# Operand sums of seven half-size products moved from GpSimd to VectorE and made earlier; weight splits moved ahead of conversions

## The chip, the cores and the metric

The kernel runs on one core of a Trainium2 chip. The metric is device time in microseconds (us) for one execution. PE is TensorE's matmul side, PEld its weight loads, DVE is VectorE, ACT is ScalarE, POOL is GpSimd, SP is the engine whose queue issues the transfers.

## The reference

Four sequences of 448 rows pass through an attention of 12 heads with two mixing matrices over the heads, and its result x (4 x 448 x 768) through a mixer:

```python
xt = x.transpose(0, 2, 1)
h = np.maximum(xt @ w_tok1, 0.0) @ w_tok2          # mixes the 448 rows
u = x + h.transpose(0, 2, 1)
h2 = np.maximum(u @ w_ch1, 0.0) @ w_ch2            # 768 -> 1536 -> 768
return (u + h2)
```

The four weights come as 64-bit floats. Only the last two products, with `w_ch1` and `w_ch2`, are touched here. Over the 4 x 448 = 1792 rows they are done in two ways: the first 768 rows directly, the last 1024 by seven half-size products in place of eight (a scheme of the Strassen and Winograd kind).

## The kernel before, in words

**Exactness.** TensorE multiplies rounded operands. Every operand is therefore kept as a pair: a rounded high part, made by a copy on ACT, and a low part, source minus high part, made by a subtraction on DVE or POOL. One product is three matmuls (`mm3`, L653 to L655): high x high, weights' high x data's low, weights' low x data's high. In the rows `wh`, `wl` are the two parts of weights and `uh`, `ul`, `rh`, `rl` those of data.

**Conversion of weights.** The 64-bit weights are turned into 32-bit ones by `cv_tick`, one unit of 128x384 at a time: absolute value on ACT (L432), clamp on POOL (L438), three bit operations on DVE (L456, L460, L466). `split` (L404) then makes the pair of 128x768 weights; if the units that it needs aren't converted yet, it runs their ticks first.

**The direct passes (L889 to L921).** Outer loop g: pass 0 has 512 rows, pass 1 has 256. Inner loop c over 12 slices of the hidden size 1536: `ch1(g, c)` is six `mm3` into `pc`, followed by relu and split of the result on ACT (`rh`, L649) and DVE (`rl`, L650); `ch2(g, c - 1)` is six more `mm3`, into six accumulators `po`. Number n = 2c is the weight pair of `ch1`, n = 2c + 1 that of `ch2`; a pair has the slot n mod 6, and its split waits until the product six numbers earlier has been done. In pass 0 the odd-numbered splits are on POOL. Conversions run only in pass 0.

**The seven products (L922 to L933).** The 1024 rows are cut into two halves, the weights into quadrants A, the data into quadrants B. There are 28 stages of 27 matmuls each (nine `mm3` of 512 columns): stages 0 to 13 are the first layer (twice the seven products in the order 1, 5, 6, 3, 7, 2, 4), stages 14 to 27 the second (each product in two parts). Products 5, 6, 3, 7 need a sum or difference of two weight quadrants (128x1152), products 5, 6, 7, 4 one of two data quadrants (128x1536). Most are made in place, in `wt`, `us` or `rr`. `prep_s(n)` issues for stage n the sums (POOL, L809), the two roundings (ACT, L835) and the two low parts (DVE, L836). High and low parts lie in one of three slots, n mod 3. The loop issues `prep_s(n + 2)`, then the matmuls of stage n, then its eviction: ACT copies, or three DVE adds (L886, L877), the former followed by relus on ACT (L864) at the head of the next turn. `prep_s(0)` and `prep_s(1)` are issued near the end of pass 1.

**Order of the work.** Every engine takes its instructions in the order in which the code issues them, and an instruction that waits holds all that are behind it on its engine. There is no scheduler.

Of the kernel before, what the change touches and what calls it, by code (L numbers as in the profile page):

```python
# [14 lines left out]
ALU = mybir.AluOpType  # L15
# [16 lines left out]
NC = DC // 128  # L32
# [7 lines left out]
def attn_mixer_kernel(  # L40
# [12 lines left out]
    nc = tc.nc  # L53
# [17 lines left out]
    def close(*names):  # L71
        for n in names:
            opens.pop(n).release()
# [23 lines left out]
    for b in range(B):  # L97
        for t in range(4):
            n = IT[t][1]
# [39 lines left out]
    def pair(tag, name):  # L139
        return (ps if tag == "pre" else ps_w).tile([128, 2, 512], F32, tag=tag, bufs=2, name=name)  # L140
# [144 lines left out]
    p = pair("w", "pw")  # L285
# [4 lines left out]
    for x in range(2):  # L290
        ps_ = slice(64 * x, 64 * x + 64)
        nc.vector.tensor_tensor(
            out=kpre[ps_, :60].rearrange("p (i g) -> p i g", i=5),
            in0=kcat[0][ps_, :12].unsqueeze(1).to_broadcast([64, 5, H]),
            in1=mask[0][ps_, 5 * x:5 * x + 5].unsqueeze(2).to_broadcast([64, 5, H]), op=ALU.mult,
# [3 lines left out]
    for s in range(2):  # L299
        ps_ = slice(64 * s, 64 * s + 64)  # L300
        for hf in range(2):
            nc.gpsimd.tensor_tensor(
                out=kpost[ps_, 32 * hf:32 * hf + 30].rearrange("p (g i) -> p g i", g=6),
                in0=kcat[1][ps_, 12 + 6 * hf:18 + 6 * hf].unsqueeze(2).to_broadcast([64, 6, 5]),
                in1=mask[1][ps_, 5 * s:5 * s + 5].unsqueeze(1).to_broadcast([64, 6, 5]), op=ALU.mult,
# [96 lines left out]
    SP, split_at = {}, [0]  # L402

    def split(eng):  # L404
        n = split_at[0]
        split_at[0] += 1
        c, w = divmod(n % (2 * NC), 2)
        while cv_pos[0] <= min(4 * c + 2 * w + 5, len(units) - 1):
            cv_tick(1)
        src = WT[w, c // 3][:, c % 3, :]  # L410
        hi, lo = [y[:, :768] for y in wslot(n % 6)]
        nc.scalar.copy(out=hi, in_=src)
        eng.tensor_tensor(out=lo, in0=src, in1=f32(hi), op=ALU.subtract)  # L413
        SP[n] = (hi, lo)

    def wslot(i):
        p = prep["wr"] if i < 3 else prep["wx"]
        return [p.tile([128, 1152 if i < 3 else 768], F32R, tag=f"w{y}{i}", name=f"w{y}") for y in "hl"]

    def xslot(i):  # L420
        return [prep["ub"].tile([128, 1536], F32R, tag=f"u{y}{i}", name=f"u{y}") for y in "hl"]

    def cv_load(i):
        src, P, n, _ = units[i]
        r = prep["cv"].tile([128, n, 2], I32, tag="cv_r", bufs=5, name="cv_r")
        nc.sync.dma_start(out=r[:P], in_=src.rearrange("p (n two) -> p n two", two=2))
        raws[i] = r

    def cv_abs(i):
        _, P, n, _ = units[i]  # L430
        g = prep["cv"].tile([128, n], F32, tag="cv_g", bufs=3, name="cv_g")
        nc.scalar.activation(out=g[:P], in_=f32(raws[i])[:P, :, 1], func=ACTF.Abs)  # L432
        mags[i] = g

    def cv_clamp(i):
        P = units[i][1]
        g = mags[i]
        nc.gpsimd.tensor_scalar(  # L438
            out=g[:P], in0=g[:P], scalar1=MAG_MIN, scalar2=MAG_MAX, op0=ALU.max, op1=ALU.min,
        )  # L440
# [30 lines left out]
    def cv_tick(k, eng=nc.gpsimd):  # L471
        for _ in range(k):
            i = cv_pos[0]
            if i >= cv_lim[0]:
                return
            if i + 5 < len(units):
                cv_load(i + 5)
            cv_step(i, eng)
            if 0 <= i + 2 < len(units):
                cv_clamp(i + 2)  # L480
            if 0 <= i + 3 < len(units):
                cv_abs(i + 3)
            cv_pos[0] += 1
# [9 lines left out]
    for T in range(NT - 1):  # L493
        J = (sl[T] + 1) // 2
        n = sf[T + 2] // 2 - J
        if sf[T + 2] % 2 and sf[T + 2] // 2 > (sf[NT - 1] - 8) // 2:
            n += 1
        n = min(3, n)
# [4 lines left out]
    for T in range(2, NT):  # L503
        hi = (sf[T] - 8) // 2
        lo = max((sl[T - 2] - 8) // 2 + 1 + (T == 4), hi - 2)
# [146 lines left out]
    def mm3(p, a, x, first, last, on=False):  # L652
        nc.tensor.matmul(out=p, lhsT=a[0], rhs=x[0], start=first, stop=False, skip_group_check=on)  # L653
        nc.tensor.matmul(out=p, lhsT=a[0], rhs=x[1], start=False, stop=False, skip_group_check=on)  # L654
        nc.tensor.matmul(out=p, lhsT=a[1], rhs=x[0], start=False, stop=last, skip_group_check=on)  # L655
# [125 lines left out]
    def ch2(g, c, ds=range(KD)):  # L781
        i0, n = CB[g]
        ws = SP[2 * NC * g + 2 * c + 1]
        for d in ds:
            if c == 0:
                OP[g, d] = psb.tile([128, 512], F32, tag=f"o{d}", name=f"po{d}")
            mm3(OP[g, d][:, :n], [w[:, 128 * d:128 * d + 128] for w in ws], RL[g, c], c == 0, c == NC - 1)
            if c == NC - 1:
                o = UR[g][:, d, :n]
                nc.vector.tensor_tensor(out=o, in0=OP.pop((g, d))[:, :n], in1=o, op=ALU.add)  # L790
                o_row[0] = d
                store_out(i0, o)


    HN = (B * S - SB0) // 2
    ORDER = [1, 5, 6, 3, 7, 2, 4]
    stages = [(0, g, p, 0) for g in range(2) for p in ORDER] + [(1, 0, p, h) for p in ORDER for h in range(2)]
    SX, SW = {}, {}
# [6 lines left out]
        t, d = (us, 3 * j) if L == 0 else (rr, 6 * j + 3 * s)  # L805
        return t[:, d:d + 3, HN * k:HN * k + HN]

    def sum_(out, in0, in1, op=ALU.subtract):
        nc.gpsimd.tensor_tensor(out=out, in0=in0, in1=in1, op=op)  # L809

    def prep_s(n):
        L, g, p, h = stages[n]
        whi, wlo = [y.rearrange("p (a n) -> p a n", a=3) for y in wslot(n % 3)]
        xhi, xlo = [y[:, :3 * HN].rearrange("p (a n) -> p a n", a=3) for y in xslot(n % 3)]
        s = g if L == 0 else h
        A = {(i, j): a_q(L, i, j, s) for i in range(2) for j in range(2)}
        Bq = {(j, k): b_q(L, j, k, h) for j in range(2) for k in range(2)}
        tmp = rr[:, 6 + 3 * g:9 + 3 * g, :HN] if L == 0 and p in (7, 4) else None
        w, x = {1: (A[0, 0], Bq[0, 0]), 2: (A[0, 1], Bq[1, 0]), 3: (A[0, 0], Bq[1, 1]), 4: (A[1, 1], tmp or Bq[1, 0]),
                5: (A[1, 0], Bq[0, 1]), 6: (A[1, 0], Bq[0, 1]), 7: (A[1, 0], tmp or Bq[0, 0])}[p]  # L820
        if p == 5:
            sum_(w, A[1, 0], A[1, 1], ALU.add)
            sum_(x, *((Bq[0, 1], Bq[0, 0]) if L or g == 0 else (Bq[1, 1], Bq[0, 1])))
        elif p == 6:
            sum_(w, A[1, 0], A[0, 0])
            sum_(x, Bq[1, 1], Bq[0, 1])
        elif p == 3:
            sum_(w, A[0, 1], A[1, 0])
        elif p == 7:
            sum_(w, A[1, 1], A[1, 0])  # L830
            sum_(x, Bq[0, 1], Bq[0, 0])
        elif p == 4:
            sum_(x, Bq[1, 0], Bq[0, 1])
        for hi, lo, src in ((whi, wlo, w), (xhi, xlo, x)):
            nc.scalar.copy(out=hi, in_=src)  # L835
            nc.vector.tensor_tensor(out=lo, in0=src, in1=f32(hi), op=ALU.subtract)  # L836
        SW[n], SX[n] = (whi, wlo), (xhi, xlo)

    PB = {}

# [25 lines left out]
    def evict(n):  # L866
# [5 lines left out]
        for m in range(3):  # L872
# [12 lines left out]
            else:  # L885
                nc.vector.tensor_tensor(out=o, in0=ps_, in1=o, op=ALU.add)  # L886
                RELU.append(o)

    for g in range(2):  # L889
        for c in range(NC):  # L890
            ch1(g, c)
            cv_tick(3)
            if g == 0 and c == NC - 3:
                cv_tick(1000)
                close("cv", "a1")
                usp = en("us", bufs=1, side="right")
                urp = en("urp", bufs=1)
                us = usp.tile([128, KD, 2 * HN], F32, name="us")
                load_u(0)
                load_u(1)  # L900
                nc.sync.dma_start(out=us, in_=u_dr[:, :, SB0:])
            if c and (g == 0 or c < NC - 1):
                ch2(g, c - 1)
            while split_at[0] < min(2 * (NC * g + c) + 6, 4 * NC):
                split(nc.gpsimd if g == 0 and split_at[0] % 2 else nc.vector)
            if g and c == NC - 2:
                prep_s(0)
        if g == 0:
            n = CB[1][1]
            U[1] = [y[:, :KD * n] for y in xslot(2)]  # L910
            hi, lo = [y.rearrange("p (d n) -> p d n", d=KD) for y in U[1]]
            nc.scalar.copy(out=hi, in_=UR[1])
            nc.vector.tensor_tensor(out=lo, in0=UR[1], in1=f32(hi), op=ALU.subtract)
            ch2(g, NC - 1)
        else:
            prep_s(1)
            ch2(g, NC - 2, (0, 1))
            for d in range(KD):
                ch2(g, NC - 1, (d,))
                if d + 2 < KD:  # L920
                    ch2(g, NC - 2, (d + 2,))  # L921
    close("psb", "urp", "ob", "wx")  # L922
    rp = en("rr", bufs=1)
    rr = rp.tile([128, NC, 2 * HN], F32, name="rr")
    pss = en("pss", bufs=1, space=PSUM)
    for n in range(len(stages)):
        relus()
        if n + 2 < len(stages):
            prep_s(n + 2)
        mm_s(n)  # L930
        evict(n)
        if n == 13:
            nc.sync.dma_start(out=us[:, :3, HN:], in_=u_dr[:, :3, SB0 + HN:])  # L933
# [39 lines left out]
```

## Time and profile before

| | us |
|---|---|
| median of 3 runs | 743.91 (742.12 to 745.80) |
| the profiled execution: device time | 742.89 |
| its span, first to last instruction | 741.1 |
| PE busy in the span | 709.5 (96%) |
| DVE busy | 596.1 (80%) |
| POOL busy | 446.4 (60%) |
| ACT busy | 392.9 (53%) |

The stretches that matter here, counted from the start of the span: pass 0 from 386 to 488, pass 1 from 488 to 540, the seven products from 540 to the end. A matmul's end is modelled in the trace and overlaps the next one, so on PE the distance from start to start tells more than the busy time.

### The profile page before, as it was taken

The numbers are of one execution on the slowest core, as the hardware profiler recorded it, in microseconds if no ns is written. First come the engines' busy times: TensorE is split into PE (matmuls) and PEld (weight loads), VectorE is DVE, ScalarE is ACT, GpSimd is POOL, SyncE is SP. The second block draws the span as 40 slices with busy tenths as digits, with TensorE's granted clock in tenths as the row PEclk, the third lists the DMA queues.
The fourth block names the chain that finished last, engine by engine and source line by source line (L and its number), as shares of the span: only waits on it lengthen the run. The fifth ranks groups of instructions, "written<-read, shape, count | busy, mean of one in ns | idle before, by whom it ended". The sixth has DMA issues, their size and how long they took to land.

```text
span 741.1 us, 19026 instructions
## 1 busy us (share of the span) xinstructions
PE 709.5 (96%) x7688; PEld 491.0 (66%) x7688; DVE 596.1 (80%) x832; ACT 392.9 (53%) x751; POOL 446.4 (60%) x291
## 2 busy tenths in 40 slices
PE   8999999999999999999999999999999979897997
PEld 4244454445445344699997888899987757685786
DVE  4777777787767879797888999865789789899992
ACT  3676666666676575464424444444554554634240
POOL 3555656665656678665657999611297297299330
PEclk9999999999999999999999999999999999999999
DMA  6788688577757644746764556750010001000022
GB/s 181 244 233 222 216 223 228 178 225 225 217 187 237 204 145 156 268 147 205 253 201 140 149 149 171 239 188 2 1 42 1 1 0 43 0 1 0 11 75 86
DMA packets 72023, 105.47 MB, mean 142 GB/s; under 512 B 23123, under 2 KB 59520, under 8 KB 71936
## 3 DMA queue, kind: packets, MB, share of 16 engines
q1 hardware_dynamic: 71360, 103.35, 45.0%
q8 instruction: 61, 1.00, 0.5%
q10 hardware_dynamic: 480, 0.87, 0.5%
q14 instruction: 26, 0.21, 0.1%
q0 software_dynamic: 96, 0.03, 0.0%
HBM read 49.18 MB, written 16.52 MB: 89 GB/s over the span
## 4 chain that ended last, share of the span: by engine, by line
PE 67%; DVE 18%; issue 7%; ACT 3%; POOL 3%; DMA 1%; SPq 0%; DVEq 0%; POOLq 0%; ACTq 0%
PE pre L174 9%; PE qk L152 9%; PE av L243 9%; PE post L214 9%; DVE ul L836 6%; DVE wl L836 4%; PE pc L655 3%; PE pc L654 3%; PE pc L653 3%; PE po L654 3%; PE po L653 3%; PE po L655 3%; DVE at L228 2%; PE pt L653 2%; PE pt L655 2%
## 5 line engine op out<-in xcount | busy, mean ns | idle before, releaser
L205 POOL TENSOR_TENSOR e<-e,sm 128x896 f32<-128x896 f32 x90 | 149.5, 1679 | 76.7 <-DVE sm L203 52.8
L158 ACT COPY s<-qk 120x896 f32<-120x896 f32 (+1 forms) x90 | 80.8, 905 | 88.0 <-PE qk L152 77.0
L191 ACT ACTIVATE e<-pre,sm 128x448 f32<-128x448 f32 x180 | 111.8, 636 | 13.9 <-DVE sm L182 9.0
L228 DVE STREAM_TRANSPOSE at<-post 128x896 f32<-128x896 f32 (+1 forms) x98 | 99.4, 1025 | 18.4 <-PE post L214 18.3
L182 DVE TENSOR_REDUCE sm<-pre 128x2 f32<-128x896 f32 x90 | 94.7, 1076 | 8.3 <-PE pre L174 8.3
L152 PE MATMUL qk<-k,q 64*64 64x448 f32 (+2 forms) x768 | 88.8, 541 | 3.6 <-DVE sm L200 2.4
L174 PE MATMUL pre<-r,kpre 64*64 64x448 f32 (+1 forms) x720 | 89.7, 553 | 2.0 <-ACT e L191 1.4
L438 POOL TENSOR_SCALAR cv_g<-cv_g 128x384 f32<-128x384 f32 (+1 forms) x52 | 82.5, 1602 | 10.5 <-ACT cv_g L432 10.4
L243 PEld LDWEIGHTS av<-at,v 64*64 64x64 f32 x2688 | 71.2, 132 | 21.0 <-ACT s L158 11.6
L836 DVE TENSOR_TENSOR wl<-wt,wh 128x1152 fp32r<-128x1152 f32 x28 | 67.0, 2393 | 18.5 <-ACT wh L835 18.5
L214 PE MATMUL post<-e,kpost 64*32 64x448 f32 x1440 | 81.2, 551 | 0.5 <-DVE at L228 0.2
L243 PE MATMUL av<-at,v 64*64 64x120 f32 (+1 forms) x2688 | 76.1, 258 | 0.6 <-ACT s L158 0.4
L654 PE MATMUL psx<-ul,wh 128*128 128x512 f32 x144 | 58.1, 403 | 6.5 <-DVE ul L836 6.5
L174 PEld LDWEIGHTS pre<-r,kpre 64*64 64x64 f32 (+1 forms) x720 | 23.7, 132 | 58.7 <-ACT e L191 30.1
L653 PE MATMUL psx<-uh,wh 128*128 128x512 f32 x144 | 57.6, 400 | 4.9 <-DVE rr L886 3.4
L152 PEld LDWEIGHTS qk<-k,q 64*64 64x64 f32 (+2 forms) x768 | 27.2, 128 | 51.0 <-DVE sm L200 25.2
L809 POOL TENSOR_TENSOR wt<-wt,wt 128x1152 f32<-128x1152 f32 x10 | 40.2, 4028 | 30.0 <-DVE wl L836 30.0
L835 ACT CAST wh<-wt 128x1152 fp32r<-128x1152 f32 x28 | 32.4, 1155 | 47.8 <-POOL wt L809 15.6
L655 PE MATMUL psx<-uh,wl 128*128 128x512 f32 x144 | 57.5, 400 | 0.0
L251 POOL COPY x<-y 128x240 f32<-128x240 f32 (+1 forms) x48 | 28.5, 598 | 41.3 <-DVE y L250 35.4
L432 ACT ACTIVATE cv_g<-cv_r 128x384 f32<-128x384 f32 (+1 forms) x52 | 28.4, 546 | 42.7 <-DVE wt L460 35.3
L655 PE MATMUL pc<-uh,wl 128*128 128x512 f32 (+1 forms) x144 | 49.3, 342 | 1.8 <-DVE wl L413 1.8
(112 smaller groups left out, 1608.4 us busy)
## 6 DMA issues: line engine op xcount, KB each, us to landing
r<-s SPq DMA_DIRECT2D x172, 210.0 KB
cv_r<-in_w_ch_dram SPq DMA_DIRECT2D x48, 384.0 KB
xr<-x_dr SPq DMA_DIRECT2D x8, 672.0 KB
u_dr<-u SPq DMA_DIRECT2D x24, 224.0 KB
k<-in_k_dram SPq DMA_DIRECT2D x20, 224.0 KB
x_dr<-x SPq DMA_DIRECT2D x36, 120.0 KB
q<-in_q_dram SPq DMA_DIRECT2D x22, 180.0 KB
v<-in_v_dram SPq DMA_DIRECT2D x16, 192.0 KB
```

Source lines behind the costliest of these rows:

```text
L152: nc.tensor.matmul(out=p[c:c + m, s, :S], lhsT=Q[T][r, h, c:c + m], rhs=K[b][r, h, :], start=True, stop=True)
L174: nc.tensor.matmul(out=p[64 * s:64 * s + 64, x, :S], lhsT=kpre[k], rhs=rt[a % NR][k], start=True, stop=True)
L182: nc.vector.tensor_reduce(out=s[:m, 0:2], in_=PP[st[0]][:m, :, :S], axis=AX.X, op=ALU.max, negate=True)
L191: nc.scalar.activation(out=E[st[0]][:m, x, :], in_=p[:m, x, :S], func=ACTF.Exp, bias=s[:m, x:x + 1], scale=1.0, accum_out=s[:m, 2 + 2 * x: ...
L205: nc.gpsimd.tensor_tensor(out=e[:m], in0=e[:m], in1=w.to_broadcast([m, 2, S]), op=ALU.mult)
L214: nc.tensor.matmul(out=p[32 * a:32 * a + 32, s, :S].rearrange("p (x g r) -> p x g r", x=2, r=32), lhsT=kpost[k, 32 * hf:32 * hf + 32], rhs ...
L228: nc.vector.transpose(out=AT[T][:, c:c + s1 - s0, :], in_=p[:, s0:s1, :S],)
L243: nc.tensor.matmul(out=p[64 * s:64 * s + 64, u, :10 * w], lhsT=V[b][k, h, j // 2 + JT * (j % 2), :], rhs=at_[k, :w, :, 32 * j + 5 * h:32 * ...
L653: nc.tensor.matmul(out=p, lhsT=a[0], rhs=x[0], start=first, stop=False, skip_group_check=on)
L654: nc.tensor.matmul(out=p, lhsT=a[0], rhs=x[1], start=False, stop=False, skip_group_check=on)
L655: nc.tensor.matmul(out=p, lhsT=a[1], rhs=x[0], start=False, stop=last, skip_group_check=on)
L836: nc.vector.tensor_tensor(out=lo, in0=src, in1=f32(hi), op=ALU.subtract)
```

## The change

`prep_s` is taken apart. `sum_w` and `sum_x` make the sums, now with DVE instructions. `split_s` makes the roundings and low parts, for weights or data or both, both roundings ahead of both low parts. In the seven products the order in a turn stays sums, split, matmuls, eviction, all for stage n + 2. The sums and splits of stages 0 and 1 are spread over pass 1 by the table `AHEAD` (at turn c = 5 the data split of stage 0, and so on), and those of stage 2 are issued in the last turn of pass 1 instead of at the head of the products. In the direct passes one of the two weight splits of a turn is moved ahead of that turn's conversions, and one of the three conversion ticks behind the second split; in the first turn one split moves from POOL to DVE.

```diff
-    def sum_(out, in0, in1, op=ALU.subtract):
-        nc.gpsimd.tensor_tensor(out=out, in0=in0, in1=in1, op=op)
-    def prep_s(n):
...
-        for hi, lo, src in ((whi, wlo, w), (xhi, xlo, x)):
-            nc.scalar.copy(out=hi, in_=src)
-            nc.vector.tensor_tensor(out=lo, in0=src, in1=f32(hi), op=ALU.subtract)
+    def sum_w(n):
+        A, _, w, _ = sources(n)
+        p = stages[n][2]
+        if p in (5, 6, 3, 7):
+            a, b = {5: (A[1, 0], A[1, 1]), 6: (A[1, 0], A[0, 0]), 3: (A[0, 1], A[1, 0]), 7: (A[1, 1], A[1, 0])}[p]
+            nc.vector.tensor_tensor(out=w, in0=a, in1=b, op=ALU.add if p == 5 else ALU.subtract)
+    def sum_x(n):
...
+            nc.vector.tensor_tensor(out=x, in0=a, in1=b, op=ALU.subtract)
+    def split_s(n, what="wx"):
...
+        for hi, lo, src in parts:
             nc.scalar.copy(out=hi, in_=src)
+        for hi, lo, src in parts:
             nc.vector.tensor_tensor(out=lo, in0=src, in1=f32(hi), op=ALU.subtract)
...
+    AHEAD = {5: [(split_s, 0, "x")], 6: [(sum_x, 1)], 7: [(sum_w, 1)], 8: [(split_s, 1, "x")], 9: [(split_s, 0, "w")],
+             10: [(split_s, 1, "w")]}
     for g in range(2):
         for c in range(NC):
             ch1(g, c)
-            cv_tick(3)
+            if split_at[0] < 2 * (NC * g + c) + 5 and split_at[0] < 4 * NC:
+                split(nc.vector)
+            cv_tick(2)
...
             while split_at[0] < min(2 * (NC * g + c) + 6, 4 * NC):
                 split(nc.gpsimd if g == 0 and split_at[0] % 2 else nc.vector)
-            if g and c == NC - 2:
-                prep_s(0)
+            cv_tick(1)
+            if g:
+                for f, *a in AHEAD.get(c, ()):
+                    f(*a)
...
-            prep_s(1)
             ch2(g, NC - 2, (0, 1))
             for d in range(KD):
                 ch2(g, NC - 1, (d,))
                 if d + 2 < KD:
                     ch2(g, NC - 2, (d + 2,))
+                if d < 2:
+                    (sum_w, sum_x)[d](2)
+            split_s(2)
...
     for n in range(len(stages)):
         relus()
-        if n + 2 < len(stages):
-            prep_s(n + 2)
+        if 2 < n + 2 < len(stages):
+            sum_w(n + 2)
+            sum_x(n + 2)
+            split_s(n + 2)
```

First place: DVE in the second layer of the seven products, the preparation of product 6 (both parts) and the eviction behind it. Before (a number behind a name tells buffers apart):

```order
L836 TENSOR_TENSOR wl<-wt_4778,wh 128x1152
L836 TENSOR_TENSOR ul<-rr,uh 128x1536
L836 TENSOR_TENSOR wl<-wt_5618,wh 128x1152
L836 TENSOR_TENSOR ul<-rr,uh 128x1536
L877 TENSOR_TENSOR us<-psz_7817,us 128x512
L877 TENSOR_TENSOR us<-psz_7818,us 128x512
L877 TENSOR_TENSOR us<-psz_7819,us 128x512
```

Now, at the same place:

```order
L823 TENSOR_TENSOR wt_4778<-wt_4778 128x3x384
L831 TENSOR_TENSOR rr<-rr 128x3x512
L843 TENSOR_TENSOR wl<-wt_4778,wh 128x1152
L843 TENSOR_TENSOR ul<-rr,uh 128x1536
L823 TENSOR_TENSOR wt_5618<-wt_5618 128x3x384
L831 TENSOR_TENSOR rr<-rr 128x3x512
L843 TENSOR_TENSOR wl<-wt_5618,wh 128x1152
L843 TENSOR_TENSOR ul<-rr,uh 128x1536
L883 TENSOR_TENSOR us<-psz_7817,us 128x512
L883 TENSOR_TENSOR us<-psz_7818,us 128x512
L883 TENSOR_TENSOR us<-psz_7819,us 128x512
```

Four sums that stood on POOL stand on DVE ahead of the low parts of their own stage.

Second place: DVE in pass 1, turns 5 to 7. Before:

```order
L413 TENSOR_TENSOR wl<-wt_5620,wh 128x768
L650 SCALAR_TENSOR_TENSOR rl<-pc_6807,rh 128x256
L413 TENSOR_TENSOR wl<-wt_5619,wh 128x768
L413 TENSOR_TENSOR wl<-wt_5620,wh 128x768
L650 SCALAR_TENSOR_TENSOR rl<-pc_6856,rh 128x256
L413 TENSOR_TENSOR wl<-wt_5621,wh 128x768
L413 TENSOR_TENSOR wl<-wt_5622,wh 128x768
```

Now:

```order
L413 TENSOR_TENSOR wl<-wt_5620,wh 128x768
L843 TENSOR_TENSOR ul<-us,uh 128x1536
L650 SCALAR_TENSOR_TENSOR rl<-pc_6811,rh 128x256
L413 TENSOR_TENSOR wl<-wt_5619,wh 128x768
L413 TENSOR_TENSOR wl<-wt_5620,wh 128x768
L831 TENSOR_TENSOR us<-us 128x3x512
L650 SCALAR_TENSOR_TENSOR rl<-pc_6861,rh 128x256
L413 TENSOR_TENSOR wl<-wt_5621,wh 128x768
L413 TENSOR_TENSOR wl<-wt_5622,wh 128x768
L823 TENSOR_TENSOR wt_5619<-wt_5619 128x3x384
```

One low part or one sum a turn has come between the second weight split and the next `rl`.

Third place: DVE in pass 0, from the `rl` of turn 6 on. Before:

```order
L650 SCALAR_TENSOR_TENSOR rl<-pc_6232,rh 128x512
L456 TENSOR_SCALAR cv_g<-cv_g 128x384
L460 SCALAR_TENSOR_TENSOR wt_5621<-cv_r,cv_g 128x384
L466 SCALAR_TENSOR_TENSOR wt_5621<-cv_r,wt_5621 128x384
L456 TENSOR_SCALAR cv_g<-cv_g 128x384
L460 SCALAR_TENSOR_TENSOR wt_5622<-cv_r,cv_g 128x384
L466 SCALAR_TENSOR_TENSOR wt_5622<-cv_r,wt_5622 128x384
L456 TENSOR_SCALAR cv_g<-cv_g 128x384
L460 SCALAR_TENSOR_TENSOR wt_5622<-cv_r,cv_g 128x384
L466 SCALAR_TENSOR_TENSOR wt_5622<-cv_r,wt_5622 128x384
L413 TENSOR_TENSOR wl<-wt_5621,wh 128x768
```

Now:

```order
L650 SCALAR_TENSOR_TENSOR rl<-pc_6240,rh 128x512
L456 TENSOR_SCALAR cv_g<-cv_g 128x384
L460 SCALAR_TENSOR_TENSOR wt_5622<-cv_r,cv_g 128x384
L466 SCALAR_TENSOR_TENSOR wt_5622<-cv_r,wt_5622 128x384
L413 TENSOR_TENSOR wl<-wt_5621,wh 128x768
L456 TENSOR_SCALAR cv_g<-cv_g 128x384
L460 SCALAR_TENSOR_TENSOR wt_5622<-cv_r,cv_g 128x384
L466 SCALAR_TENSOR_TENSOR wt_5622<-cv_r,wt_5622 128x384
```

The weight split of DVE has moved ahead of all but one of the turn's four conversions; the number of conversions in the turn is the same.

## Rows read from the trace of the kernel before

**Rows 1.** Busy time by stretch: pass 0, pass 1, the seven products.

```profile
core 0: us, PE busy (x) PEld busy (x) DVE busy (x) ACT busy (x) POOL busy (x), PEclk, DMA share, GB/s
386.00:488.00 102.00, 100.21 (x436) 82.44 (x434) 88.10 (x129) 43.63 (x70) 80.56 (x45) 0.98 0.59 181
488.00:540.50 52.50, 52.31 (x434) 51.94 (x433) 38.04 (x44) 24.88 (x36) 8.49 (x3) 1.00 0.10 31
540.50:741.10 200.60, 180.03 (x758) 144.34 (x756) 168.44 (x98) 88.06 (x94) 119.91 (x30) 0.97 0.07 24
```

**Rows 2.** Waits of PE, 540 to 737: us in total, times, longest.

```profile
PE psx L654 <- DVE ul L836: 6.5, 4, 2.8
PE psz L654 <- DVE ul L836: 5.1, 4, 2.3
PE psx L653 <- DVE rr L886: 3.4, 3, 2.8
PE psx L653 <- ACT rr L882: 1.4, 1, 1.4
```

**Rows 3.** Timeline of PE (start, duration): first and last matmuls of the products.

```profile
540.46 0.40 PE L653 MATMUL psx<-uh,wh 128*128 128x512 f32 x1
...
735.24 0.39 PE L655 MATMUL psx<-uh,wl 128*128 128x512 f32 x1
...
736.60 0.39 PE L655 MATMUL psx<-uh,wl 128*128 128x512 f32 x1
```

**Rows 4.** DVE's low parts by form, 540.5 to 741.1: count, busy, mean ns, idle before.

```profile
L836 DVE TENSOR_TENSOR wl<-wt,wh 128x1152 fp32r<-128x1152 f32 x26 | 64.3, 2472 | 17.2 <-ACT wh L835 17.2
L836 DVE TENSOR_TENSOR ul<-rr,uh 128x1536 fp32r<-128x1536 f32 x18 | 49.6, 2756 | 0.0
L836 DVE TENSOR_TENSOR ul<-us,uh 128x1536 fp32r<-128x1536 f32 x9 | 33.1, 3676 | 0.7 <-ACT uh L835 0.7
```

**Rows 5.** Timeline of DVE in the products.

```profile
551.87 3.83 DVE L836 TENSOR_TENSOR wl<-wt,wh 128x1152 fp32r<-128x1152 f32 x1
555.62 5.05 DVE L836 TENSOR_TENSOR ul<-us,uh 128x1536 fp32r<-128x1536 f32 x1
...
573.41 3.69 DVE L836 TENSOR_TENSOR wl<-wt,wh 128x1152 fp32r<-128x1152 f32 x1 [1.75 <-ACT wh L835]
...
582.31 1.36 DVE L836 TENSOR_TENSOR wl<-wt,wh 128x1152 fp32r<-128x1152 f32 x1 [1.74 <-ACT wh L835]
583.69 1.76 DVE L836 TENSOR_TENSOR ul<-us,uh 128x1536 fp32r<-128x1536 f32 x1
585.36 1.88 DVE L886 TENSOR_TENSOR rr<-psz,rr 128x512 f32<-128x512 f32 x3
```

**Rows 6.** Timeline of POOL in the products.

```profile
550.41 4.08 POOL L809 TENSOR_TENSOR wt<-wt 128x1152 f32<-128x1152 f32 x1
554.45 4.62 POOL L809 TENSOR_TENSOR rr<-us 128x1536 f32<-128x1536 f32 x1
...
590.43 4.22 POOL L809 TENSOR_TENSOR wt<-wt,wt 128x1152 f32<-128x1152 f32 x1 [14.54 <-DVE wl L836]
```

**Rows 7.** Timeline of PE in pass 0.

```profile
398.75 0.39 PE L654 MATMUL pc<-ul,wh 128*128 128x512 f32 x1
400.93 0.50 PE L655 MATMUL pc<-uh,wl 128*128 128x512 f32 x1 [1.79 <-DVE wl L413]
...
402.19 0.61 PE L654 MATMUL pc<-ul,wh 128*128 128x512 f32 x1
...
405.58 0.41 PE L653 MATMUL pc<-uh,wh 128*128 128x512 f32 x1
...
471.81 0.39 PE L654 MATMUL po<-rl,wh 128*128 128x512 f32 x1
```

**Rows 8.** Timeline of DVE in pass 0, turn 9.

```profile
467.54 2.08 DVE L466 SCALAR_TENSOR_TENSOR wt<-cv_r,wt 128x384 uint32<-128x384 uint32 x1
469.55 0.68 DVE L650 SCALAR_TENSOR_TENSOR rl<-pc,rh 128x512 fp32r<-128x512 f32 x1
```

**Rows 9.** Timeline of DVE in pass 1, under the two sums of stage 1.

```profile
520.31 4.80 DVE L413 TENSOR_TENSOR wl<-wt,wh 128x768 fp32r<-128x768 f32 x2
```

More of the change, by code (lines that the diff above doesn't have):

```diff
@@ L806, in b_q, with sources @@
         return t[:, d:d + 3, HN * k:HN * k + HN]
-    def sum_(out, in0, in1, op=ALU.subtract):
-        nc.gpsimd.tensor_tensor(out=out, in0=in0, in1=in1, op=op)
-    def prep_s(n):
+    def sources(n):
         L, g, p, h = stages[n]
-        whi, wlo = [y.rearrange("p (a n) -> p a n", a=3) for y in wslot(n % 3)]
-        xhi, xlo = [y[:, :3 * HN].rearrange("p (a n) -> p a n", a=3) for y in xslot(n % 3)]
         s = g if L == 0 else h
@@ L820, in prep_s @@
                 5: (A[1, 0], Bq[0, 1]), 6: (A[1, 0], Bq[0, 1]), 7: (A[1, 0], tmp or Bq[0, 0])}[p]
[L821 to L833, printed above, removed]
-        for hi, lo, src in ((whi, wlo, w), (xhi, xlo, x)):
+        return A, Bq, w, x
+    def sum_w(n):
[5 more added lines that the diff above has]
+    def sum_x(n):
+        _, Bq, _, x = sources(n)
+        L, g, p, h = stages[n]
+        if p in (5, 6, 7, 4):
+            a, b = {5: (Bq[0, 1], Bq[0, 0]) if L or g == 0 else (Bq[1, 1], Bq[0, 1]), 6: (Bq[1, 1], Bq[0, 1]),
+                    7: (Bq[0, 1], Bq[0, 0]), 4: (Bq[1, 0], Bq[0, 1])}[p]
+            nc.vector.tensor_tensor(out=x, in0=a, in1=b, op=ALU.subtract)
+    def split_s(n, what="wx"):
+        t = {"w": (SW, wslot, 384), "x": (SX, xslot, HN)}
+        parts = []
+        for y in what:
+            to, slot, m = t[y]
+            to[n] = [z[:, :3 * m].rearrange("p (a n) -> p a n", a=3) for z in slot(n % 3)]
+            parts.append((*to[n], sources(n)["wx".index(y) + 2]))
+        for hi, lo, src in parts:
             nc.scalar.copy(out=hi, in_=src)
+        for hi, lo, src in parts:
             nc.vector.tensor_tensor(out=lo, in0=src, in1=f32(hi), op=ALU.subtract)
-        SW[n], SX[n] = (whi, wlo), (xhi, xlo)
     PB = {}
```

## The prediction

> **What bounds the kernel now.** I read the busy time by stretch first, then TensorE's waits in the stretch with the largest idle share, then the instructions that end those waits.
>
> By stretch [rows 1] the reader is to see three different states. In pass 0 and pass 1 PE is busy nearly all the time (100.2 of 102.0 us, 52.3 of 52.5). In the seven products it is busy 180.0 of 200.6, with DVE at 168.4 and POOL at 119.9. PE's work is fixed by the change, so what can be won is the time that PE loses, and nearly all of it lies in the products. Its size: the last matmuls start 0.227 us apart (six between 735.24 and 736.60) [rows 3], and 28 stages of 27 are 756, which is 171.4 us. From the first start at 540.46 to the last at 736.60 plus 0.23 are 196.4 [rows 3]. **25.0 us are lost.** The waits by name give 16.4 of them [rows 2]: 11.6 for a low part of data, 3.4 for an eviction on DVE, 1.4 for one on ACT that stood behind a sum. The other 8.6 are restarts and matmuls at 1.2 GHz: the granted clock of this stretch is 0.97 on the mean, where it is 1.00 in pass 1 [rows 1].
>
> Why are the low parts late? The same subtraction takes 1.36 us (weights) and 1.76 (data) at 582 to 585, where POOL stands idle (it waited 14.54 us before 590.43), and 3.83 and 5.05 at 551.87 and 555.62, where POOL is making a sum [rows 5, 6]. There each low part ends just behind the sum that ran beside it: the sum ends at 550.41 + 4.08 = 554.49, the low part at 555.70; the next sum at 559.07, the next low part at 560.67. So the low part does not run slowly, it stands until the sum is through and then takes 1.2 to 1.6 us, its time alone. Over the stretch 53 low parts take 147.0 us [rows 4], a mean of 2.77 against 1.56 alone. DVE and POOL do this work one after the other, and DVE's in-order queue carries the delay to PE.
>
> The Trainium skill, page "SBUF — State Buffer", section "Who interferes with whom", says that a VectorE instruction with two SBUF inputs and a GpSimd instruction that reads SBUF exclude each other for a whole instruction. The rows above agree: 1.2 and 1.6 us behind the sum's end.
>
> **The change part by part.**
>
> *Sums to DVE, in the products.* Removed from POOL: 30 sums in the stretch [rows 1], and with them every overlap. The low parts should fall to 1.36 and 1.76. Added to DVE: for stages 3 to 27, 14 sums of weights and 14 of data. No row shows a sum on DVE. The nearest rows are the low parts, the same kind of instruction with the same shapes and two SBUF inputs: from start to start 1.38 (582.31 to 583.69) and 1.67 (583.69 to 585.36) [rows 5]. Bounds: these as the lower end, since a sum can't do with less than one of equal size; the overlapped 3.83 and 5.05 as the upper. I take the lower end, because the rows that are longer all have a POOL sum beside them and none will be left. The sums are 14 x 1.38 + 14 x 1.67 = 42.7 us.
>
> What DVE then needs per product, with 3.05 for a pair of low parts, 3.05 for a pair of sums, 1.88 for three adds of an eviction [rows 5]. First layer, once through the seven: product 1 3.05, 5 and 6 6.10 each, 3 6.31, 7 7.98, 2 4.93, 4 4.72, together 39.2 against PE's 7 x 6.12 = 42.8. Second layer, both parts: 1 and 2 7.98 each, 5, 6 and 7 14.08 each, 3 10.74, 4 11.32, together 80.3 against 85.7. Over the 28 stages DVE has 158.7; stages 0 to 2 are made beforehand (three pairs of low parts, two of sums: 15.3), which leaves 143.4 against 171.4 of PE. To this come hand-offs: six times DVE waits 1.75 for the rounding that stands behind the relus on ACT [rows 5], 10.5. So **PE becomes the bound of the stretch, with DVE at 154 of 171.**
>
> Locally DVE is overloaded. Products 5 and 6 of the second layer need 14.08 each where PE needs 12.24: 3.7 us are lost over the two, 1.5 come back in product 3, and 1.8 go in product 7. The reserve is small, since the low parts of stage n + 2 wait for the slot that stage n - 1 frees. I followed the three queues stage by stage with the durations above (each instruction starts when its engine and its inputs are free): low parts are ready 3 to 6 us before PE wants them through the first layer, 3.4 at the start of the second, nothing at product 3; PE then waits 0.9, 1.6 and 0.1. **2.6 us of the 25.0 stay.** Each tenth of a microsecond more per hand-off adds about 3.6 to it, and 5% longer DVE instructions add 3.9.
>
> *Sums and splits in pass 1.* POOL's two sums there go, and with them low parts of 4.80 for two [rows 9]. DVE gets five or six instructions of 1.4 to 1.8 earlier. DVE is busy 38.0 of 52.5 us and ACT 24.9 [rows 1]; per turn of 4.4 us at most one of them is added, and `rl`, which stands behind it, is read a whole `ch2` and `ch1` later. Cost nothing, hidden under PE's matmuls; if that cover failed, at most one such instruction a turn would show, 6 x 1.8 = 11 us. The sums of stage 2 stand between evictions of the last accumulators; their banks are wanted by stage 1, 6 us later.
>
> *Splits ahead of conversions, pass 0.* One stall goes: PE waits at 398.98 for a weight split that stands behind three conversions, until 400.93, and eight matmuls from 402.19 to 405.58 then take 0.424 each instead of 0.227 [rows 7] (TensorE at 1.2 GHz, the lower of its two levels, behind a wait; 0.227 is at 2.4): 1.95 + 1.58 = 3.5 us. But DVE doesn't get less to do in this pass, it gets one split more (0.95). By turn 9 `rl` ends at 469.55 + 0.68 = 470.23, and the matmul that reads it starts at 471.81 [rows 7, 8]. That reserve of 1.6 exists because PE had lost 3.5 before. With PE 3.5 earlier and DVE 0.9 later it is -2.8, so PE stalls late in the pass by that much. Net gain 0.7. Bounds: the whole 3.5 if DVE's overlaps with POOL's splits (a bit operation of 2.08 at 467.54 [rows 8]) fall kinder, and a loss of 3 if the new order adds hand-offs to ACT.
>
> *The sum.* 742.89 for the profiled execution, minus 25.0, plus 2.6, minus 0.7 is 719.8. The median of the runs is 743.91, 1.0 above that execution, so the median should be **721**.
>
> **The rivals.**
>
> *All stalls go* (the best case): no reserve runs out, pass 0 keeps its 3.5: 743.9 - 25.0 - 3.5 = 715. For it: DVE's 154 against 171. Against: products 5, 6 and 7 of the second layer. Chance 0.15.
>
> *DVE sets the pace of the second layer.* Hand-offs of 0.15 us in place of 0.03, or sums 5 to 10% longer than the low parts, make PE wait 7 to 11 us there in place of 2.6, some of it with matmuls at 1.2 GHz as after 402 [rows 7]: 725 to 733. For it: every split is a chain of sum, rounding on ACT, low part, with no work of another stage between. Against: in 582 to 590 the same chains cost no more than 1.75 [rows 5]. Chance 0.24.
>
> *Slower: the low parts keep their length.* If the 2.77 were DVE's own (strided quadrants, say) and not POOL's doing, the sums would come on top: 168.4 + 42.7 + 17.9 of waits for ACT [rows 1, 4] is 229 against 200.6, so 771. It decides by the low parts' mean: DVE's slack now is 200.6 - 168.4 - 17.9 = 14.3, so they must fall by 42.7 - 14.3 = 28.4 in 53, from 2.77 to 2.24, or time is lost. For it: DVE is the busier of the two already. Against: 1.36 and 1.76 wherever POOL rests [rows 5, 6]. Chance 0.04.
>
> The Trainium skill, page "Perfetto Trace Analysis", section "Optimizing Scalar/DVE Operations", says that where DVE is saturated, work may be offloaded to GpSimd, which speaks against this change; it adds that the two share a read port, so that it might not help. By its first half the time would be that rival's 771; the trace bears out the second half.
>
> *No effect*: PE's waits have another cause that stays, 741 to 746. Against it, all four rows of waits end in DVE or in what stood behind a sum [rows 2]. Chance 0.04.
>
> **How the numbers follow.** My forecast, 717.5 to 725, has 0.53. The range for 8 in 10 takes in the best case and most of the second rival: 714.5 to 732. A measurement of this kernel can tell about 0.5%, 3.7 us, from no change. Faster by more: 0.53 + 0.15 + 0.24 = 0.92. Within: 0.04. Slower by more: 0.04.
>
> **What would show it.** In the changed profile: low parts in the products at 1.36 and 1.76 throughout, sums on DVE at the same; POOL at zero there; PE's waits in the first layer gone, 2 to 3 us left around products 5 to 7 of the second; the granted clock 1.00 in that stretch; in pass 0 no wait near 399, but waits for `rl` late in the pass. I am wrong if sums on DVE take clearly over 1.4 and 1.7, if DVE is busy over 171 us of the products, or if pass 1 shows PE waiting.

## The result: 719.85 us in place of 744.72

The changed kernel takes 719.85 us (median of 4 runs, 719.64 to 721.38), the kernel before, run beside it, 744.72 (4 runs). The ratio is 0.9675, with a 95% interval from 0.9645 to 0.9706. The prediction was 721. The profiled execution of the changed kernel took 721.38 us, the longest of the four, so between the two profiles 742.89 - 721.38 = 21.5 us are to be explained.

Busy time by stretch after the change (pass 0, pass 1, the products), with the columns of [rows 1]:

```profile
386.00:484.00 98.00, 93.74 (x410) 76.36 (x409) 88.49 (x130) 42.45 (x68) 73.30 (x43) 1.00 0.60 175
484.00:537.00 53.00, 52.89 (x417) 51.56 (x416) 36.59 (x44) 26.87 (x37) 1.86 (x1) 1.00 0.16 58
537.00:719.60 182.60, 177.55 (x801) 146.87 (x800) 151.23 (x129) 90.31 (x95) 0.00 (x0) 1.00 0.08 26
```

In the third row POOL is at zero and the granted clock at 1.00, where [rows 1] had 119.91 and 0.97. In the first PE lacks 4.3 of 98.0 us.

Waits of PE from 380 us to the end, answering [rows 2] (us in total, times, longest):

```profile
PE po L654 <- DVE rl L650: 4.3, 4, 1.2
PE psx L654 <- DVE ul L843: 0.9, 1, 0.9
PE pt L653 <- DVE u L686: 0.2, 1, 0.2
```

The 16.4 us of waits of [rows 2] are down to 0.9. New are four waits in pass 0 for `rl`. First and last matmul of the products, answering [rows 3]:

```profile
542.58 0.40 PE L653 MATMUL psx<-uh,wh 128*128 128x512 f32 x1
...
715.11 0.39 PE L655 MATMUL psx<-uh,wl 128*128 128x512 f32 x1
```

From the first start to the last plus 0.23 are 172.8 us, where there were 196.4: 23.6 won, and 1.4 left above the 171.4 of the matmuls. The first start lies 2.1 later than in [rows 3]. 23.6 - 2.1 is the 21.5.

DVE's sums (L823, L831) and low parts (L843) in the products by form, answering [rows 4]; smaller groups are left out:

```profile
L843 DVE TENSOR_TENSOR wl<-wt,wh 128x1152 fp32r<-128x1152 f32 x27 | 36.5, 1353 | 16.7 <-ACT wh L841 16.5
L843 DVE TENSOR_TENSOR ul<-rr,uh 128x1536 fp32r<-128x1536 f32 x18 | 31.6, 1758 | 3.7 <-ACT uh L841 3.5
L843 DVE TENSOR_TENSOR ul<-us,uh 128x1536 fp32r<-128x1536 f32 x8 | 14.1, 1758 | 0.7 <-ACT uh L841 0.6
L831 DVE TENSOR_TENSOR rr<-rr 128x1536 f32<-128x1536 f32 x8 | 14.0, 1749 | 0.0
L823 DVE TENSOR_TENSOR wt<-wt,wt 128x1152 f32<-128x1152 f32 x10 | 13.5, 1349 | 0.0
```

Low parts that took 2.47, 2.76 and 3.68 us on the mean [rows 4] take 1.35 and 1.76, and a sum takes what a low part of its size takes. So DVE gained 28 sums in the products and still has less to do there: the 53 low parts shown went from 147.0 to 82.2 us.

DVE in pass 0. First the kernel before, the turn that ends with the `rl` of [rows 8]: the `rl` that opens the turn, and the first step of its last conversion:

```profile
460.18 0.68 DVE L650 SCALAR_TENSOR_TENSOR rl<-pc,rh 128x512 fp32r<-128x512 f32 x1
...
466.56 0.35 DVE L456 TENSOR_SCALAR cv_g<-cv_g 128x384 uint32<-128x384 uint32 x1
```

Then two turns of the changed kernel, and POOL in the same time:

```profile
460.08 2.00 DVE L456 TENSOR_SCALAR cv_g<-cv_g 128x384 uint32<-128x384 uint32 x1
...
463.37 0.68 DVE L650 SCALAR_TENSOR_TENSOR rl<-pc,rh 128x512 fp32r<-128x512 f32 x1
463.97 0.35 DVE L456 TENSOR_SCALAR cv_g<-cv_g 128x384 uint32<-128x384 uint32 x1
...
469.78 2.01 DVE L456 TENSOR_SCALAR cv_g<-cv_g 128x384 uint32<-128x384 uint32 x1
...
473.07 0.68 DVE L650 SCALAR_TENSOR_TENSOR rl<-pc,rh 128x512 fp32r<-128x512 f32 x1
```

```profile
459.74 2.13 POOL L413 TENSOR_TENSOR wl<-wt,wh 128x768 fp32r<-128x768 f32 x1 [1.44 <-ACT wh L412]
...
469.43 2.14 POOL L413 TENSOR_TENSOR wl<-wt,wh 128x768 fp32r<-128x768 f32 x1 [1.45 <-ACT wh L412]
```

The conversion step L456 takes 0.35 us by itself and 2.0 where POOL has its split: it ends 0.2 behind the split. DVE's turn, from `rl` to `rl`, is 473.07 - 463.37 = 9.70; before it was 469.55 - 460.18 = 9.37. PE at the end of the second of these turns:

```profile
472.17 0.39 PE L653 MATMUL po<-rh,wh 128*128 128x512 f32 x1
473.80 0.50 PE L654 MATMUL po<-rl,wh 128*128 128x512 f32 x1 [1.24 <-DVE rl L650]
```

It starts as `rl` ends (473.07 + 0.68), 1.63 after the matmul before it.

### The profile page after: what moved, and what is told of

It is laid out like the page before. It is cut to its first block, busy times and chain, and to the rows that moved or that the text cites. A ratio compares the mean times of both kernels' runs of the same rounds, so it can differ in the third digit from the quotient of the medians.

```text
span 719.6 us, 18988 instructions
## 1 busy us (share of the span) xinstructions
PE 699.5 (97%) x7688; PEld 486.7 (68%) x7688; DVE 577.2 (80%) x865; ACT 395.9 (55%) x751; POOL 312.6 (43%) x258
## 4 chain that ended last, share of the span: by engine, by line
PE 74%; DVE 16%; issue 5%; ACT 2%; DMA 1%; SPq 1%; POOL 0%; DVEq 0%; ACTq 0%; POOLq 0%
PE pre L174 9%; PE qk L152 9%; PE post L214 9%; PE av L243 9%; PE psx L654 5%; PE psx L655 5%; PE psx L653 4%; DVE cv_g L456 4%; DVE wt L460 3%; PE psz L653 3%; PE psz L654 3%; PE psz L655 3%; DVE at L228 2%; PE pt L653 2%; PE pt L654 2%
## 5 line engine op out<-in xcount | busy, mean ns | idle before, releaser
L438 POOL TENSOR_SCALAR cv_g<-cv_g 128x384 f32<-128x384 f32 (+1 forms) x52 | 79.6, 1546 | 10.8 <-ACT cv_g L432 10.7
L654 PE MATMUL psx<-ul,wh 128*128 128x512 f32 x144 | 56.3, 391 | 0.9 <-DVE ul L843 0.9
L653 PE MATMUL psx<-uh,wh 128*128 128x512 f32 x144 | 56.1, 389 | 0.0
L655 PE MATMUL psx<-uh,wl 128*128 128x512 f32 x144 | 56.0, 389 | 0.0
L654 PE MATMUL po<-rl,wh 128*128 128x512 f32 (+1 forms) x144 | 49.0, 340 | 4.3 <-DVE rl L650 4.3
L843 DVE TENSOR_TENSOR wl<-wt,wh 128x1152 fp32r<-128x1152 f32 x28 | 37.9, 1354 | 16.8 <-ACT wh L841 16.5
L412 ACT CAST wh<-wt 128x768 fp32r<-128x768 f32 x48 | 39.6, 831 | 19.5 <-PE po L654 11.0
L654 PE MATMUL pc<-ul,wh 128*128 128x512 f32 (+1 forms) x144 | 48.5, 337 | 0.1
```

## The experiments

The theory: (1) the products' gain comes from taking GpSimd's reading instructions away from beside DVE's; (2) the new order in pass 0 costs time, since the split left on GpSimd now holds a dearer DVE instruction. The main rivals: DVE's order, the earlier start or POOL's mere activity made the gain; pass 0 is worth nothing either way. Each ratio is against the kernel before, run on the same chip in the same job. The changed kernel again:

> The changed kernel once more, for comparison on the same chip: 719 to 721.5 us.

Measured: 721.85 us, 0.9705 (0.9681 to 0.9728). The gain repeats, 0.35 above the range that was expected; this is the level that the next ones are held against.

**The old order in the direct passes, sums on DVE kept.**

```diff
-            if split_at[0] < 2 * (NC * g + c) + 5 and split_at[0] < 4 * NC:
-                split(nc.vector)
-            cv_tick(2)
+            cv_tick(3)
...
-            cv_tick(1)
```

> Undoes the order of splits and conversions in the two direct passes; sums on DVE and the work made ahead stay. Theory (VectorE sets the pace of pass 0, so the moved split only changes which stall is paid): the 3.5 us stall near 399 comes back and the four waits for rl (4.3 us, 5.3 with restarts) go, so 1 to 2 us faster than the changed kernel, 718 to 719. Rival (moving the split is a gain of its own): 2 to 4 us slower, 722 to 724.

Measured: 719.66, 0.9669 (0.9649 to 0.9690), 2.2 us under the changed kernel of the same job. PE's waits:

```profile
PE pc L655 <- DVE wl L413: 1.8, 1, 1.8
PE psx L654 <- DVE ul L843: 0.9, 1, 0.9
```

The wait near 399 [rows 7] is back, the four for `rl` are gone, and the whole is faster, by about what was expected (719.66 lies a little above the 718 to 719). So the whole gain comes from the sums on DVE and their earlier start, none of it from the order in the direct passes.

**The new order alone, in the kernel before** (the same lines the other way round):

> The kernel before with only the order of splits and conversions in the direct passes changed; sums stay on GpSimd. Theory (VectorE's pace in pass 0): the wait near 399 goes, waits for rl of about 4.3 us come, 0.5 to 2.5 us slower than before, ratio 1.000 to 1.004. Rival (a gain of its own): 2 to 4 us faster, ratio 0.995 to 0.997.

Measured: 745.44, 1.0035 (1.0016 to 1.0055). The four waits for `rl` appear as in the changed kernel (4.3 us). The two halves multiply to the whole: 1.0035 x 0.9669 = 0.970.

**The sums back on GpSimd, all else as changed.**

```diff
-            nc.vector.tensor_tensor(out=w, in0=a, in1=b, op=ALU.add if p == 5 else ALU.subtract)
+            nc.gpsimd.tensor_tensor(out=w, in0=a, in1=b, op=ALU.add if p == 5 else ALU.subtract)
```

(and the same in `sum_x`)

> The changed kernel's order and its work made ahead, but the 32 sums on GpSimd again. Theory (a sum on GpSimd and a low part on VectorE exclude each other): low parts of the products back to a mean near 2.8 us, 736 to 743 us. Rival (it was the earlier order, both roundings ahead of both low parts, that paid): 719 to 726.

Measured: 741.52, 0.9967 (0.9947 to 0.9987). Low parts in the products by form:

```profile
L843 DVE TENSOR_TENSOR wl<-wt,wh 128x1152 fp32r<-128x1152 f32 x26 | 60.9, 2341 | 20.6 <-ACT wh L841 20.6
L843 DVE TENSOR_TENSOR ul<-rr,uh 128x1536 fp32r<-128x1536 f32 x18 | 49.6, 2756 | 0.1
L843 DVE TENSOR_TENSOR ul<-us,uh 128x1536 fp32r<-128x1536 f32 x8 | 30.5, 3808 | 0.7 <-ACT uh L841 0.7
```

They are back at their old length. So the early start and the new order within a stage are not what shortens them; the engine of the sums is. Against the 1.0035 of the new order alone, 0.9967 leaves some 5 us, give or take 2, for the early start and the order of the roundings together, with the sums on GpSimd; the two were not taken apart.

**GpSimd reads beside DVE.** In the changed kernel GpSimd makes, from stage 16 on, one idle subtraction in scratch memory for each sum of the stage; nobody uses what it writes.

```diff
...
+        nc.scalar.copy(out=tiny, in_=t[:, 0, :1])
+        for k, ps_ in ((384, (5, 6, 3, 7)), (512, (5, 6, 7, 4))):
+            if p in ps_:
+                s = t[:, :, :k]
+                nc.gpsimd.tensor_tensor(out=s, in0=sc[2][:, :, :k], in1=sc[2][:, :, :k], op=ALU.subtract)
...
+            if n + 2 > 15:
+                dummy(n + 2)
```

(The first five lines are the body of `dummy`; `sc` are weight tiles that are no longer used.)

> The changed kernel with 16 idle sums on GpSimd added in the second layer of the products (two inputs and one output of 128x1152 or 128x1536, in weight tiles no longer used, results not used), each started when ScalarE has made the roundings of a stage, so beside its low parts. Theory (a GpSimd instruction that reads SBUF and a VectorE one with two SBUF inputs exclude each other): low parts and sums on VectorE to 3 to 5 us wherever they meet, 735 to 760 us. Rival (slow low parts had another cause): 719 to 722.

Measured: 742.13, 0.9985 (0.9960 to 1.0011): sixteen instructions whose results nobody uses take back all that was won. DVE and POOL beside each other:

```profile
645.40 7.41 POOL L950 TENSOR_TENSOR wt<-wt 128x1152 f32<-128x1152 f32 x2 [3.36 <-ACT tiny L946]
...
650.14 4.30 DVE L831 TENSOR_TENSOR rr<-rr 128x1536 f32<-128x1536 f32 x1
...
654.36 1.34 DVE L843 TENSOR_TENSOR wl<-wt,wh 128x1152 fp32r<-128x1152 f32 x1
```

A sum of 1.75 takes 4.30: GpSimd's subtractions end at 652.81, the sum 1.63 later. The next instruction, with GpSimd at rest, takes its 1.34.

**GpSimd writes beside DVE.** The same with three fills in place of each subtraction:

```diff
-                nc.gpsimd.tensor_tensor(out=s, in0=sc[2][:, :, :k], in1=sc[2][:, :, :k], op=ALU.subtract)
+                [nc.gpsimd.memset(s, 0.0) for _ in range(3)]
```

> As the one before, but with three fills of zeros on GpSimd in place of each idle sum, which only write SBUF. Theory (only reading excludes): low parts stay at 1.36 and 1.76, 719 to 723 us. Rival (any GpSimd access to SBUF excludes): 735 to 760 us, as with the idle sums.

Measured: 719.80, 0.9689 (0.9663 to 0.9715), no cost. GpSimd and DVE from 626 us on:

```profile
L950 POOL MEMSET wt<- 128x1536 f32 x24 | 33.3, 1386 | 7.6 <-ACT tiny L946 6.4
...
L843 DVE TENSOR_TENSOR ul<-rr,uh 128x1536 fp32r<-128x1536 f32 x13 | 22.8, 1757 | 2.7 <-ACT uh L841 2.7
...
L831 DVE TENSOR_TENSOR rr<-rr 128x1536 f32<-128x1536 f32 x8 | 14.0, 1752 | 0.0
```

GpSimd is busy 58.8 us in that time as against 59.0 with the subtractions (the small copy on ACT that starts it is in both), and DVE's instructions keep their length. So a GpSimd that merely runs, or writes, doesn't hold DVE here, and one that subtracts, and so reads, does. The Trainium skill, page "SBUF — State Buffer", section "Who interferes with whom", says just this of a VectorE instruction with two SBUF inputs: GpSimd's reads hold it, its writes don't. These two runs agree, with 4.30 against 1.75; GpSimd's clamps, which read SBUF too, do not (last section).

**The sums of stages 0 to 2 not made ahead**, but each two stages before its use, as in the kernel before:

```diff
-            if g:
-                for f, *a in AHEAD.get(c, ()):
-                    f(*a)
+            if g and c == NC - 2:
+                prep_n(0)
...
+            prep_n(1)
...
-        if 2 < n + 2 < len(stages):
+        if n + 2 < len(stages):
+            prep_n(n + 2)
```

(`prep_n` calls `sum_w`, `sum_x` and `split_s`; the calls for stage 2 in the last turn are gone.)

> The changed kernel, sums on VectorE, but sums and splits of stages 0 to 2 at the places that they had before. Theory (TensorE bounds the products, and VectorE has 3 to 6 us of reserve in the first layer): at most 2 us slower than the changed kernel, 720 to 723. Rival (making them ahead carries much of the gain, since VectorE has about 6 us more to do in the stretch and starts it late): 725 to 735.

Measured: 724.49 (721.55 to 725.02), 0.9746 (0.9717 to 0.9774), in the job of which 0.9705 would be 721.1: about 3 us worse, between what the two expected. The two intervals just touch. DVE at the seam between pass 1 and the products:

```profile
538.89 1.35 DVE L843 TENSOR_TENSOR wl<-wt,wh 128x1152 fp32r<-128x1152 f32 x1
540.52 1.76 DVE L843 TENSOR_TENSOR ul<-us,uh 128x1536 fp32r<-128x1536 f32 x1 [0.28 <-ACT uh L841]
542.20 2.08 DVE L790 TENSOR_TENSOR ur<-po,ur 128x256 f32<-128x256 f32 x6
```

The evictions of the last accumulators (L790) stand behind stage 1's preparation, and PE waits 1.45 us for them at 542.67; two more waits for `ul` (1.3 and 0.6) follow. So the early part is worth some 3 us by the ratios; the profiled execution was the fastest of the four, so how the 3 us divide over these waits stays open.

**How much room DVE has.** The low part of the data is made twice in stages 3 to 27 (25 instructions of 1.67 from start to start, 41.8 us):

```diff
         for hi, lo, src in parts:
             nc.vector.tensor_tensor(out=lo, in0=src, in1=f32(hi), op=ALU.subtract)
+        if n > 2:
+            nc.vector.tensor_tensor(out=lo, in0=src, in1=f32(hi), op=ALU.subtract)
```

> The changed kernel with the low part of the data made twice over in stages 3 to 27 (25 instructions of 1.67 us more on VectorE, 41.8 us). Theory (VectorE has 154 of 171 us in the products, so TensorE is the bound by 17 us and no more): VectorE becomes the bound, and all above its slack shows, 20 to 35 us slower than the changed kernel, 740 to 755. Rival (VectorE has far more slack than that sum says, since its queue also waits): under 12 us slower, 722 to 732.

Measured: 755.95, 1.0157 (1.0128 to 1.0185), just above the top of what was expected. Against the changed kernel's 0.9705 of the same 744.43, 722.5, this is 33.5 us more. The products' stretch:

```profile
542.00:755.40 213.40, 183.85 (x763) 145.24 (x762) 190.42 (x149) 89.17 (x94) 0.00 (x0) 0.96 0.07 22
```

Only about 8 of 41.8 us found cover, where 171 - 154 had promised 17. DVE is busy 190 of 213 even when it sets the pace: of the other 23, some 15 go in waiting for roundings, which a sum of busy times doesn't count as load. Part of the 33.5 is also that PE, now stopping often, has a granted clock of 0.96.

**All weight splits of the direct passes on DVE**, in the new order:

```diff
-                split(nc.gpsimd if g == 0 and split_at[0] % 2 else nc.vector)
+                split(nc.vector)
```

> The changed kernel with all weight splits of pass 0 on VectorE, none on GpSimd. Theory (each split on GpSimd holds VectorE for 1.65 us, a conversion step of 2.00 instead of 0.35, which is more than the 0.95 that the split itself costs there): turn of VectorE from 9.7 to about 8.9 us, no waits for rl, 714.5 to 717. Rival (VectorE is simply overloaded in pass 0, more work makes it later): turn of 10.6 us, 724 to 728.

Measured: 715.37, 0.9609 (0.9585 to 0.9633). Only the 0.9 in the products is left of PE's waits. DVE in pass 0 by form, in the changed kernel:

```profile
L456 DVE TENSOR_SCALAR cv_g<-cv_g 128x384 uint32<-128x384 uint32 x34 | 26.5, 781 | 0.0
L466 DVE SCALAR_TENSOR_TENSOR wt<-cv_r,wt 128x384 uint32<-128x384 uint32 x34 | 23.5, 692 | 1.2
...
L413 DVE TENSOR_TENSOR wl<-wt,wh 128x768 fp32r<-128x768 f32 x13 | 12.9, 992 | 0.1
```

and with all splits on DVE:

```profile
L413 DVE TENSOR_TENSOR wl<-wt,wh 128x768 fp32r<-128x768 f32 x25 | 23.9, 964 | 3.4 <-PE po L655 2.4 <-ACT wh L412 1.0
L460 DVE SCALAR_TENSOR_TENSOR wt<-cv_r,cv_g 128x384 uint32<-128x384 uint32 x34 | 20.6, 607 | 1.2
L466 DVE SCALAR_TENSOR_TENSOR wt<-cv_r,wt 128x384 uint32<-128x384 uint32 x35 | 19.5, 558 | 1.2
L456 DVE TENSOR_SCALAR cv_g<-cv_g 128x384 uint32<-128x384 uint32 x34 | 16.5, 486 | 0.0
```

DVE makes twelve splits more (+11.0 us) and is done sooner: L456 and L466 fall by 14.0. Its turn is 441.37 - 432.42 = 8.95 us, as expected:

```profile
432.42 0.68 DVE L650 SCALAR_TENSOR_TENSOR rl<-pc,rh 128x512 fp32r<-128x512 f32 x1
...
441.37 0.68 DVE L650 SCALAR_TENSOR_TENSOR rl<-pc,rh 128x512 fp32r<-128x512 f32 x1
```

**All splits on DVE in the old order** (the old order of the first experiment and all splits on DVE as in the one above, together):

> Sums on VectorE and made ahead, all weight splits of pass 0 on VectorE, but splits behind the conversions as before the change. Theory (what pass 0 paid for was GpSimd's splits, the order is secondary): the wait near 399 stays (3 to 4 us), no waits for rl, 717 to 719.5, so slower by 2 to 4 than with the new order (715.4). Rival (the new order is a loss by itself): 713 to 715.

Measured: 714.56 (714.52 to 715.83), 0.9605 (0.9582 to 0.9629), the fastest kernel here and not to be told from the one above (0.9609). The expectation missed: the wait near 399 should have stayed, and didn't. The time lies in the range of the rival, but a loss by the order itself, without GpSimd's splits, is not shown: 0.0004 is far inside both intervals. DVE near 399 in the kernel before the change:

```profile
396.19 2.19 DVE L466 SCALAR_TENSOR_TENSOR wt<-cv_r,wt 128x384 uint32<-128x384 uint32 x1
398.31 2.57 DVE L413 TENSOR_TENSOR wl<-wt,wh 128x768 fp32r<-128x768 f32 x1
```

POOL there in the kernel before the change:

```profile
396.12 3.95 POOL L413 TENSOR_TENSOR wl<-wt,wh 128x768 fp32r<-128x768 f32 x2 [0.84 <-ACT wh L412]
```

and DVE in the last kernel:

```profile
396.17 0.56 DVE L466 SCALAR_TENSOR_TENSOR wt<-cv_r,wt 128x384 uint32<-128x384 uint32 x1
396.64 2.69 DVE L413 TENSOR_TENSOR wl<-wt,wh 128x768 fp32r<-128x768 f32 x3
```

Three splits on DVE end at 399.33 where, with two of the three on POOL, DVE's one ended at 400.88. So that stall, too, does not come without GpSimd's splits, although the three conversions stand ahead of the split as before. The new order removes it as well, but it also takes a split of the first turn from GpSimd to DVE, so what the order by itself does there is not shown.

## Why the prediction was right, and where it was not

**Low parts and sums in the products: right.** 1.36 and 1.76 were expected for low parts, 1.38 and 1.67 from start to start for sums; 1.35, 1.76 and sums of 1.35 and 1.75 came (1.27 and 1.67 from start to start). The choice of the lower bound for the sums is what carried the forecast.

**What stays of the 25.0: 2.6 expected, 1.4 measured.** The wait came at one place, not at three: it is the 0.9 at product 7 of the second layer. DVE and ACT there:

```profile
673.32 1.75 DVE L831 TENSOR_TENSOR rr<-rr 128x1536 f32<-128x1536 f32 x1
674.99 1.35 DVE L843 TENSOR_TENSOR wl<-wt,wh 128x1152 fp32r<-128x1152 f32 x1
676.70 1.76 DVE L843 TENSOR_TENSOR ul<-rr,uh 128x1536 fp32r<-128x1536 f32 x1 [0.36 <-ACT uh L841]
```

```profile
675.18 1.49 ACT L841 CAST uh<-rr 128x1536 fp32r<-128x1536 f32 x1 [0.50 <-DVE rr L831]
```

The rounding of the data starts 0.11 behind the end of the sum and takes 1.49, and DVE has only a low part of 1.35 to do meanwhile: it stands for 0.36. From the end of the rounding to the low part there are the 0.03 that the forecast had taken.

**Pass 0: the step that failed.** It was forecast as a net gain of 0.7 (3.5 for the stall that goes, 2.8 for waits on `rl` that come). The stall went and the waits came, as said, but their size was wrong: the pass lost. The first matmul of the products starts 2.1 later, of which 0.36 was there before pass 0, so the direct passes lost 1.8 between the two profiles; the medians of the runs put the loss at 1.0035 - 1 of 743 (2.6 us) and 721.85 - 719.66 (2.2). The mis-sized term is "DVE 0.9 later". It took one split of 0.95 and let the turns of DVE be as they were. In fact the `rl` of turn 9 comes 473.07 - 0.36 - 469.55 = 3.2 later, and the waits with their restarts cost about 5.3, not 2.8. The 3.2 are made up so: 0.7 are there by turn 4; 1.1 come in the turn after it, which has one conversion more than in the kernel before (9.70 in place of 8.56); 1.3 come in the four turns that follow, each 9.70 in place of 9.37. Nearly all of these 0.33 a turn lie in its last conversion, which takes 3.29 (469.78 to 473.07) where it took 2.99 (466.56 to 469.55 [rows 8]). Before, GpSimd's split fell on L466 (2.08 [rows 8] where it takes 0.56 to 0.74 otherwise); after, it falls on L456 (2.0 where it takes 0.35). PE needs 36 x 0.227 = 8.2 for a turn, so the reserve ran down in the kernel before as well; there the pass was over before it was gone. The -3 bound for "hand-offs to ACT" covered the size, not the cause. And the stall at 399 was put down to the conversions ahead of the split; the last experiment shows that it does not come without GpSimd's splits.

**Pass 1 costs nothing: right.** PE is busy 52.89 of 53.00, no wait of PE stands in it.

**DVE at 154 of 171, PE the bound: right in its outcome, wrong as a measure of room.** In the 172.8 us from the first matmul of the products to the last DVE was busy for 145.7, near the 143.4 of the forecast. But it also waited 18.7 for roundings (20.6 in the wider window of the rows by form above) where 10.5 were taken, though [rows 4] had shown 17.9 already. Together 164.4, which leaves 8.4, about the 8 that the doubling found.

**The rivals.** The slower one (low parts keep their length, 771) fell with the rows by form. The best case of 715 assumed that pass 0 keeps 3.5; what reaches 715 is another edit. "DVE sets the pace" did not come, but was nearer than the 17 us of room made it look: the waits for roundings were nearly twice what was taken, and some 8 us of room kept PE ahead. The Trainium skill, page "Perfetto Trace Analysis", section "Optimizing Scalar/DVE Operations", says that offloading from a saturated DVE to GpSimd may make sense, and then doubts it, since the two share a read port. Here the doubt was right twice, for the sums and for the splits.

**The number.** That 721 lies so near 719.85 is in part luck. Of the profiled execution, forecast at 719.8, the products took 1.2 less than forecast, pass 0 took 2.5 more, and 0.36 were lost ahead of it: 721.38. The 1.0 that was added from the profiled execution to the median had the other sign this time, -1.5.

## What to carry to other kernels

Before work is given to GpSimd, compare what it spares VectorE with what it holds VectorE up: here an instruction of 0.95 us given away cost 1.65 in the queue it was taken from, while the clamps that stayed on GpSimd cost VectorE little. Where an instruction's mean is far above the time of the same shape at another place in the trace, look at what the neighbour engine does in just that time; the engine with the longest busy time may be the one that is only standing. And where busy times show room, test it by doubling an instruction before filling it.

## What the runs showed of the hardware that was not expected

- A VectorE instruction with a single SBUF input (L456, 32-bit shift and mask, 128x384) is held by GpSimd's subtraction as well: 2.00 us in place of 0.35.
- GpSimd's clamps (L438, one input and one output in SBUF, 1.5 to 2.1 us each) hardly hold VectorE. With them alone beside it, as in the run with all splits on VectorE, L466 and L460, which have two inputs in SBUF, stay at 558 and 607 ns on the mean. One place of the run with the old order and all splits on VectorE:

```profile
456.75 3.18 POOL L438 TENSOR_SCALAR cv_g<-cv_g 128x384 f32<-128x384 f32 x2 [0.78 <-ACT cv_g L432]
...
459.39 0.56 DVE L466 SCALAR_TENSOR_TENSOR wt<-cv_r,wt 128x384 uint32<-128x384 uint32 x1
```

  So a GpSimd instruction that reads SBUF holds VectorE in some forms and not in others; which property decides was not tested.
- In the kernel before, PE stood still from 398.98 to 400.93 and a little later ran eight matmuls at 0.424 us [rows 7], with a granted clock of 0.53 from 402.0 to 405.5, the lower of its two levels (1.2 GHz). The four waits for `rl` in the changed kernel were not followed by this: the granted clock of that pass is 1.00.
